# Gating and scattering chunks 18 and 19 inside the retention of a fused retention and mixture-of-experts kernel

## The chip, the cores and the metric

The kernel runs on one core of a Trainium2 chip. The metric is the device time of one execution in microseconds, the median of several runs; lower is better.

## The reference

The program is two layers in a row. A retention layer keeps, for each of 4 batches and 8 heads, a decaying 64 x 64 state over 768 steps; its output, 3072 tokens of 512 features, goes into a mixture of 8 experts in which each token takes the one expert with the largest gate logit.

```python
for t in range(S):                       # B, H, S, D = 4, 8, 768, 64
    state = gamma * state + einsum('bhd,bhe->bhde', k[:, :, t], v[:, :, t])
    y[:, :, t] = scale * einsum('bhd,bhde->bhe', q[:, :, t], state)
x = y.transpose(0, 2, 1, 3).reshape(B * S, H * D)        # 3072 x 512
...
expert_idx = argmax(x @ w_gate, axis=1)                  # 8 experts
for e in range(E):
    xe = x[expert_idx == e]
    out[mask] = gate_w[mask, None] * (maximum(xe @ w1[e], 0) @ w2[e])
```

## The kernel before

The 3072 tokens are 24 chunks of 128 tokens. A loop over n = 0 to 11 takes two chunks, a = 2n and b = 2n + 1, at a time: TensorE (PE) multiplies scores, updates the state and forms the output, VectorE (DVE) masks the scores (`Sb`) and evicts the output (`evict`, tile `xT`), ScalarE (ACT) copies the state (`ub`) and the turned rows (`rows`, tile `xrow`), GpSimd (POOL) scales the values of a later chunk (`scale`, tile `vs`, line 258). Iteration n also makes the gate logits of the two chunks before (`logits`, `finish_logits`).

Chunks are gated in groups, `GROUPS`, each as (first chunk, number). `gating` returns the steps of one group: `choose` finds the best expert on DVE, `soft` and `weights` the gate weight, `rank` counts on PE with small matmuls how many earlier tokens chose the same expert, `slots` turns that into the row of the token in the sorted buffer (`KEY`), `label` writes weight and token number into `xrow` on ACT, `advance` adds the group to the counts that later ranks need. When `KEY` and the label are there, `send_rows` scatters a chunk, one indirect transfer issued by POOL (line 840), into `x_sorted` in DRAM, where each expert's tokens lie together. `BEHIND`, `AMID` and `AFTER` say in which iteration finished chunks are scattered; `send_behind` first copies one column of a tile on POOL (`gated`, line 354), so that POOL goes on only once that tile is written. Between two scatters stands either a `scale` or a `pause`, an idle POOL operation on 256 numbers (line 200). `FULL = 18`: after chunk 17 the expert with the most tokens is known to have enough of them. Its first 256 tokens (`EARLY`) are then fetched (`fetch_early`, tile `xg0`), turned and cut into a high and a low part (`xh0`, `xl0`; the first half of the low part on POOL, line 869). In the code a write to `x_sorted` that stands behind a read of it waits for that read, except where `disjoint` or `declare_no_dep` says otherwise; the scatters are declared free of each other, and of the fetch of the early rows they are not.

The expert weights come as 1 MB pieces (`fetch`, line 136, tile `raw`, two buffers) issued by SyncE (SP) and are split into a high and a low part (`split`, ACT for the high, POOL or DVE for the low part, lines 144 and 145). `SPLITS` places pieces of the first expert's weights in iterations 6, 7, 9, 10 and 11; in 10 and 11 the low parts are POOL's.

After the loop come 32 pieces of the early expert's two products (`early_pieces`, lines 895 and 918; `fill(n)` issues the next n). In their order, with h for a hidden block and r for a result block: h0 h0, then h h r r for each of blocks 1 to 7, then r7 r7. Among them stand, in program order, the rest of the gating, the scatters of the last chunks, the fetch of the late rows (`first["late"]`, the early expert's rows behind the first 256, tile `xg1`), `expert_at[1]`, the first weights `fetch(1, 0)` and the rows of the next expert (tile `buf`). SP then issues `fetch(1, 1)`, waits for POOL's split of `(1, 0)`, issues `fetch(1, 2)`, writes five pads (line 796), loads six registers (line 750) and issues `fetch(1, 3)`. `prep_slices` turns and cuts the late rows on DVE and ACT. Behind that, `moe_main` multiplies the late block (lines 1061 to 1078) and then expert after expert (lines 1164 and 1196). Each engine takes its instructions in the order in which the program issues them.

Of the kernel before, what the change touches and what calls it, by code (L numbers as in the profile page):

```python
# [10 lines left out]
F32 = mybir.dt.float32  # L11
# [8 lines left out]
E, DM, F = 8, 512, 1024  # L20
N = B * S
P = 128
# [21 lines left out]
MAXB = CMAX32 // 32  # L44
WARM = 8
FILL = (1, 3, 4)
GROUPS = ((0, 6), (6, 6), (12, 4), (16, 2), (18, 4), (22, 2))
FULL = 18
BEHIND = {3: (0, 1), 4: (2, 3), 5: (4, 5), 6: (6, 7), 7: (10, 11), 8: (12, 13)}
AMID = {7: (8, 9)}  # L50
AFTER = {8: (14, 15)}
PAUSE = 256
# [54 lines left out]
def retention_moe(ctx, tc, front, qkv, w1, w2, first_rows, second_rows, out):  # L107
# [39 lines left out]
    def region(which):  # L147
        if isinstance(which, int):
            return x_sorted[which]
        return x_sorted[bass.ds(which, 1)].rearrange("o n m -> (o n) m")  # L150
# [47 lines left out]
    def pause():  # L198

        nc.gpsimd.tensor_tensor(out=idle[0:1], in0=cs[0:1, 0:PAUSE], in1=cs[0:1, 0:PAUSE], op=ALU.mult)  # L200
# [19 lines left out]
    with ExitStack() as actx:  # L220
# [6 lines left out]
        ps_1 = apool("ps_1", 1, space=PS)  # L227
# [39 lines left out]
        def bank(i, name, shape=(P, NP, C)):  # L267
            return ps_s.tile(list(shape), F32, name=name, tag=f"s{i}")
# [88 lines left out]
        def send_apart(chunks, between=pause):  # L357
            for i, g in enumerate(chunks):
                if i:
                    between()  # L360
                send_rows(g)

        def send_rows(g):
            b, c = divmod(g, CPB)
            sent = scatter_rows(tc, x_rows, KEY[:, g, 0:1], xrows[b][:, c].rearrange("t q m -> t (q m)"), "sorted")
            if g < GROUPS[0][1]:
                disjoint(tc, sent, "front")
# [18 lines left out]
        def finish_logits(t):  # L386
            i = [n for n, (a, w) in enumerate(GROUPS) if a <= 2 * t < a + w][0]
            a, w = GROUPS[i]
            both = ps_1.tile([P, 2, TW], F32, name="lp", tag="misc")
# [14 lines left out]
        def gating(i):  # L404
            a, w = GROUPS[i]
            total = a + w in (GROUPS[0][1], FULL, NCH)
            last = a + w == NCH
# [4 lines left out]
            NB = w + total  # L412
            v = {}
# [22 lines left out]
                nc.scalar.activation(out=ex[:, :, 0:E], in_=v["sh"], func=AF.Exp)  # L436

            def rank():
                pf = v["pf"] = bank(2, "pf", (P, NB, E)) if i < 3 else ps_1.tile([P, NB, E], F32, name="pf", tag="U" if i == 4 else "misc")
                nc.tensor.matmul(out=pf[:, 0:w, :], lhsT=us, rhs=Eb, start=True, stop=False, skip_group_check=True)  # L440
                for part in [run] + tots:
                    nc.tensor.matmul(out=pf, lhsT=ones, rhs=part.unsqueeze(1).broadcast_to([P, NB, E]),
                                     start=False, stop=False, skip_group_check=True)
                for n in range(NB - 1):
                    nc.tensor.matmul(out=pf[:, n + 1:, :], lhsT=ones,
                                     rhs=Eb[:, n:n + 1, :].broadcast_to([P, NB - 1 - n, E]),
                                     start=False, stop=(n == NB - 2), skip_group_check=True)
# [54 lines left out]
        def fill_rows():  # L502


            assert GROUPS[0][1] * C // E <= 32 * NJ0 - P
            sent = nc.sync.dma_start(out=region(expert_at[0])[32 * NJ0 - P:32 * NJ0], in_=cs[:, 0:ROW])
# [39 lines left out]
        def fill(n):  # L546
            for _ in range(n):
                fn, a = early.pop(0)
                fn(*a)
# [53 lines left out]
        stages = {}  # L603

        for n in range(last + 1):
            a, b = 2 * n, 2 * n + 1
            s = gating(chosen[n]) if n in chosen else None
# [38 lines left out]
            if n == soon:  # L646
                for name in ("slots", "weights", "label", "counts"):
                    s[name]()
                nc.vector.tensor_copy(out=filled, in_=full)
                nc.vector.tensor_scalar(out=s0, in0=full, scalar1=base, scalar2=float(EARLY), op0=ALU.subtract,  # L650
                                        op1=ALU.min)
                nc.vector.tensor_tensor(out=start, in0=s0, in1=base, op=ALU.add)
                send_apart(range(FULL - 2, FULL))
                fill_late()
                fetch_early()
            elif s and n < last:
                s["rank"]()
                s["slots"]()
# [10 lines left out]
            if n == soon - 1:  # L669
                scale(b + 2)  # L670
                scale(a + 4)
            if n in BEHIND:
                send_behind(xTs[n][:, 0, C:C + 1], BEHIND[n], pause if n == soon - 1 else lambda: scale(b + 2))
            if n == 1:
# [19 lines left out]
            if n < last:  # L694
                if n not in BEHIND:
                    scale(b + 2)
# [10 lines left out]
                    load(i)  # L707
        mark_early()

        s = stages[4]  # L710
        fill(FILL[0])
        rows(2 * last, "U", ps_1)
        logits(last)
# [3 lines left out]
        s["rank"]()  # L717
        for name in ("slots", "weights", "advance", "label"):
            s[name]()
        send_apart(range(18, 22))  # L720
        finish_logits(last)
        final = gating(5)
        final["choose"]()
        fill(FILL[2])
        final["soft"]()
# [58 lines left out]
        nc.vector.tensor_scalar(out=mask7, in0=empty, scalar1=float(BIG), scalar2=k_("quad"),  # L784
                                op0=ALU.mult, op1=ALU.add)
        token_mask(0, late, P)
        fill(4)
        prep_slices(nc, nc.vector, xhl1[:, 0], xhl1[:, 1], xt1, xg1, 0, P)
        token_index(0)
        fill(4)  # L790
        for i in range(2):
            split(1, 0, i, nc.gpsimd)
        fetch(1, 2)
# [551 lines left out]
```

## Time and profile before

| | |
|---|---|
| median of 3 runs | 391.99 us (391.64 to 392.82) |
| profiled execution | 394.47 us |
| its span, first to last instruction | 392.7 us |
| mean granted TensorE clock | 0.985 |
| busy: PE, DVE, ACT, POOL | 377.2, 246.3, 140.6, 260.7 us |
| PE busy share of the span | 96% |

Times of instructions are microseconds from the start of the span, so a time in a row is a place in the span. Busy times of different engines lie beside each other and don't add up. The profiled execution is 1.8 us longer than its span; what lies around the span isn't seen in the trace.

### The profile page before, as it was taken

Reading aid. Unit: us, or ns where it says so; the run is one execution under the profiler, and the core shown is the slowest. Engines: PE = TensorE matmul, PEld = TensorE weight load, DVE = VectorE, ACT = ScalarE, POOL = GpSimd, SP = SyncE. Lnnn points to the kernel's source line nnn. Section 1 sums busy time; section 2 is a strip of 40 time slices with the busy share of each in tenths; the row PEclk is TensorE's granted clock in tenths of the full one; section 3 lists DMA queues with packets and bytes.
Section 4 is the critical chain, followed back from the end, with each engine's and each line's share of the span. In section 5 each row is a group of like instructions: output and inputs, shape, how many; then the busy total and the mean of one; then the engine's idle time right before and its main releaser. Section 6 shows DMA issues by size and latency. Waiting matters only on the chain.

```text
span 392.7 us, 8671 instructions
## 1 busy us (share of the span) xinstructions
PE 377.2 (96%) x3272; PEld 352.7 (90%) x3272; DVE 246.3 (63%) x483; ACT 140.6 (36%) x248; POOL 260.7 (66%) x281
## 2 busy tenths in 40 slices
PE   8999999999998998999999999999999999999991
PEld 5887888778997797899999999999999999999881
DVE  3467667765785496675875578386757649667110
ACT  2222334335331463433442353155235325424100
POOL 3752669898480749500699499849929974995874
PEclk9999999999998999899999999999999999999997
DMA  7999999965038979656572764665556455610102
GB/s 300 418 417 415 411 408 420 411 264 165 30 136 207 259 243 272 189 212 131 196 240 65 181 240 140 137 209 167 166 149 223 164 134 201 222 56 17 43 27 76
DMA packets 42030, 82.05 MB, mean 209 GB/s; under 512 B 4267, under 2 KB 17583, under 8 KB 39536
## 3 DMA queue, kind: packets, MB, share of 16 engines
q1 hardware_dynamic: 36656, 67.67, 52.9%
q0 software_dynamic: 5312, 13.49, 9.6%
q8 instruction: 47, 0.77, 0.8%
q14 instruction: 15, 0.12, 0.1%
HBM read 65.80 MB, written 15.82 MB: 208 GB/s over the span
## 4 chain that ended last, share of the span: by engine, by line
PE 69%; DMA 10%; POOL 8%; DVE 6%; issue 3%; SPq 1%; ACT 1%; POOLq 0%; DVEq 0%
PE py L1196 24%; PE ph L1164 23%; PE sp L276 5%; PE Y L326 5%; DMA out<-Z,sidx 4%; POOL out L840 4%; PE tr L346 3%; PE U L291 3%; PE Y L313 3%; DMA buf<-x_sorted 3%; POOL idle L200 2%; DVE wlo L145 2%; PE L L380 2%; DMA raw<-w 2%; DMA head<-first_rows 1%
## 5 line engine op out<-in xcount | busy, mean ns | idle before, releaser
L840 POOL DMA_INDIRECT out<-Z,sidx x88 | 100.6, 1143 | 74.1 <-DVE Z L1043 59.4
L145 DVE TENSOR_TENSOR wlo<-raw,whi 128x1024 fp32r<-128x1024 f32 (+1 forms) x61 | 72.1, 1191 | 14.4 <-ACT whi L144 14.0
L200 POOL TENSOR_TENSOR idle<-cs 1x256 bf16<-1x256 f32 x103 | 75.2, 730 | 2.9
L144 ACT CAST whi<-raw 128x1024 fp32r<-128x1024 f32 (+1 forms) x72 | 67.1, 950 | 11.0 <-DMA raw<-w 11.0
L1196 PE MATMUL py<-hh,whi 128*128 128x392 f32 (+4 forms) x192 | 66.2, 345 | 0.0
L1196 PE MATMUL py<-hh,wlo 128*128 128x392 f32 (+4 forms) x192 | 66.1, 344 | 0.0
L1196 PE MATMUL py<-hl,whi 128*128 128x392 f32 (+4 forms) x192 | 66.0, 344 | 0.0
L1171 ACT ACTIVATE hh<-ph 128x452 fp32r<-128x452 f32 (+6 forms) x56 | 28.3, 507 | 79.2 <-PE ph L1164 78.5
L1164 PE MATMUL ph<-xh,whi 128*128 128x392 f32 (+5 forms) x224 | 49.0, 341 | 2.4 <-DVE hl L1172 2.4
L1172 DVE SCALAR_TENSOR_TENSOR hl<-ph,hh 128x452 fp32r<-128x452 f32 (+6 forms) x56 | 31.9, 572 | 29.6 <-ACT hh L1171 27.9
L1164 PE MATMUL ph<-xl,whi 128*128 128x392 f32 (+5 forms) x224 | 49.6, 343 | 0.0
L1164 PE MATMUL ph<-xh,wlo 128*128 128x392 f32 (+5 forms) x224 | 49.5, 343 | 0.0
L1164 PEld LDWEIGHTS ph<-xh,whi 128*128 128x128 f32 x224 | 40.0, 188 | 3.4 <-DVE hl L1172 3.1
L1164 PEld LDWEIGHTS ph<-xl,whi 128*128 128x128 f32 x224 | 40.8, 190 | 0.2
L1164 PEld LDWEIGHTS ph<-xh,wlo 128*128 128x128 f32 x224 | 40.6, 189 | 0.2
L1196 PEld LDWEIGHTS py<-hh,whi 128*128 128x128 f32 x192 | 36.2, 189 | 0.6 <-DVE Z L1038 0.4
L1196 PEld LDWEIGHTS py<-hl,whi 128*128 128x128 f32 x192 | 36.2, 189 | 0.2
L1196 PEld LDWEIGHTS py<-hh,wlo 128*128 128x128 f32 x192 | 36.2, 189 | 0.2
L279 DVE TENSOR_TENSOR Sb<-sp,cs 128x512 f32<-128x512 f32 x48 | 30.0, 681 | 6.5 <-PE sp L276 6.5
L862 ACT CAST xh<-buf 128x512 fp32r<-128x512 f32 (+7 forms) x26 | 14.4, 556 | 53.9 <-DVE buf L855 53.9
L840 POOL DMA_INDIRECT x_sorted<-xrow,KEY x24 | 25.0, 1041 | 11.3 <-DVE mx L421 5.4
L869 DVE TENSOR_TENSOR xl<-buf,xh 128x512 fp32r<-128x512 f32 (+7 forms) x26 | 17.1, 661 | 13.7 <-ACT xh L862 12.2
(197 smaller groups left out, 557.9 us busy)
## 6 DMA issues: line engine op xcount, KB each, us to landing
raw<-w SPq DMA_DIRECT2D x32, 1024.0 KB
qkv_w<-qkv SPq DMA_DIRECT2D x12, 1024.0 KB, 17.3
qkv_t<-qkv SPq DMA_DIRECT2D x7, 1024.0 KB
qkv_t<-front SPq DMA_DIRECT2D x7, 512.0 KB, 6.3
buf<-x_sorted SPq DMA_DIRECT2D x12, 211.2 KB, 3.8
x_sorted<-cs SPq DMA_DIRECT2D x7, 260.0 KB, 6.5
buf<-x_sorted SPq DMA_DIRECT2D x8, 195.0 KB, 3.6
out<-Z,sidx POOLq DMA_INDIRECT x88
```

The source lines that it names most:

```text
L144: nc.scalar.copy(out=hi[:, h], in_=raw[:, h])
L145: engine.tensor_tensor(out=lo[:, h], in0=raw[:, h], in1=hi[:, h].bitcast(F32), op=ALU.subtract)
L200: nc.gpsimd.tensor_tensor(out=idle[0:1], in0=cs[0:1, 0:PAUSE], in1=cs[0:1, 0:PAUSE], op=ALU.mult)
L276: nc.tensor.matmul(out=sps[r][:, p, :], lhsT=kt[half[r], p, :], rhs=q[half[r], p, :], start=True, stop=True)
L279: nc.vector.tensor_tensor(out=Sb[:, r], in0=sps[r], in1=causal.unsqueeze(1).broadcast_to([P, NP, C]), op=ALU.mult)
L326: nc.tensor.matmul(out=at(Y, g, half[o], r, m), lhsT=vp[:, p, half[r]], rhs=Sb[:, r, p, :], start=(g == 0 and m == 0), stop=True, skip_gro ...
L840: sc = tc.nc.gpsimd.indirect_dma_start(out=dst, out_offset=bass.IndirectOffsetOnAxis(ap=index, axis=0), in_=rows, in_offset=None, bounds_c ...
L869: engine.tensor_tensor(out=xl[:, :, sl], in0=xt[:, :, t0:t0 + w], in1=xh[:, :, sl].bitcast(F32), op=ALU.subtract)
L1164: nc.tensor.matmul(out=ph[:, :w], lhsT=wparts[e, f // 4][a][:, kd, fo:fo + P], rhs=x[:, kd, :w], start=(n == 0), stop=(n == 3 * KD - 1))
L1171: nc.scalar.activation(out=hh[:, :cap], in_=ph[:, :cap], func=AF.Relu)
L1172: nc.vector.scalar_tensor_tensor(out=hl[:, :cap], in0=ph[:, :cap], scalar=0.0, in1=hh[:, :cap].bitcast(F32), op0=ALU.max, op1=ALU.subtract)
L1196: nc.tensor.matmul(out=py[:, :c], lhsT=a[:, f % 4, k * P:(k + 1) * P], rhs=x[:, :c], **se)
```

## The change

Three edits. Group (18, 4) becomes (18, 2) and (20, 2). The first of these is gated in iteration 10, and chunks 18 and 19 are scattered there, behind the eviction of that iteration, with `scale(23)` between them; it was gated in iteration 11 and scattered after the loop. Behind the loop only 20 and 21, and then 22 and 23, are left; since there is one group more, the last one's stage is number 6, and the banks of `rank` are named by the first chunk instead of the number. Before chunk 16 is scattered, a pause is issued. And the preparation of the late rows (`prep_slices`, `token_index`) stands four `fill` pieces earlier: ahead of r4 r4 h6 h6 instead of behind them.

```diff
-GROUPS = ((0, 6), (6, 6), (12, 4), (16, 2), (18, 4), (22, 2))
+GROUPS = ((0, 6), (6, 6), (12, 4), (16, 2), (18, 2), (20, 2), (22, 2))
 FULL = 18
-BEHIND = {3: (0, 1), 4: (2, 3), 5: (4, 5), 6: (6, 7), 7: (10, 11), 8: (12, 13)}
+BEHIND = {3: (0, 1), 4: (2, 3), 5: (4, 5), 6: (6, 7), 7: (10, 11), 8: (12, 13), 10: (18, 19)}
...
-                pf = v["pf"] = bank(2, "pf", (P, NB, E)) if i < 3 else ps_1.tile([P, NB, E], F32, name="pf", tag="U" if i == 4 else "misc")
+                pf = v["pf"] = bank(2, "pf", (P, NB, E)) if a < FULL - 2 or a == FULL else ps_1.tile([P, NB, E], F32, name="pf", tag="U" if a == FULL + 2 else "misc")
...
                 nc.vector.tensor_tensor(out=start, in0=s0, in1=base, op=ALU.add)
+                pause()
                 send_apart(range(FULL - 2, FULL))
                 fill_late()
                 fetch_early()
...
-        s = stages[4]
+        s = stages[5]
...
-        send_apart(range(18, 22))
+        send_apart(range(20, 22))
         finish_logits(last)
-        final = gating(5)
+        final = gating(6)
...
         token_mask(0, late, P)
-        fill(4)
         prep_slices(nc, nc.vector, xhl1[:, 0], xhl1[:, 1], xt1, xg1, 0, P)
         token_index(0)
-        fill(4)
+        fill(8)
```

## Rows read from the trace of the kernel before

**Rows 1.** Who waited for whom, PE alone: us in total, times, longest.

```profile
PE ph L1164 <- DVE hl L1172: 2.4, 2, 1.9
PE acc L918 <- ACT hh L903: 1.4, 1, 1.4
...
PE acc L918 <- DVE hl L904: 0.5, 1, 0.5
```

**Rows 2.** Busy time by stretch: PE, PEld, DVE, ACT, POOL, granted clock, DMA share, GB/s.

```profile
124.80:128.20 3.40, 3.40 (x13) 2.92 (x12) 1.46 (x5) 1.38 (x2) 0.24 (x1) 0.50 1.19 228
...
158.90:162.30 3.40, 3.40 (x12) 3.21 (x11) 0.08 (x1) 0.53 (x2) 3.04 (x4) 0.50 0.96 325
162.30:340.00 177.70, 177.68 (x981) 176.61 (x980) 122.52 (x177) 73.40 (x105) 116.02 (x122) 1.00 0.58 171
```

**Rows 3.** Timeline of POOL, 104 to 116: start, duration, instruction, idle before and releaser.

```profile
104.66 1.01 POOL L840 DMA_INDIRECT x_sorted<-xrow,KEY  x1 [5.39 <-DVE mx L421]
...
106.46 1.01 POOL L840 DMA_INDIRECT x_sorted<-xrow,KEY  x1 [0.16 <-issue]
...
111.92 1.27 POOL L840 DMA_INDIRECT x_sorted<-xrow,KEY  x1 [0.16 <-issue]
...
114.48 1.01 POOL L840 DMA_INDIRECT x_sorted<-xrow,KEY  x1 [0.16 <-issue]
```

**Rows 4.** Timeline of SP's queue, 117 to 145.

```profile
117.38 1.91 SPq L154 DMA_DIRECT2D xg<-x_sorted  x4
...
132.72 0.39 SPq L136 DMA_DIRECT2D raw<-w  x1
...
134.06 6.39 SPq L796 DMA_DIRECT2D x_sorted<-cs  x5
144.42 0.40 SPq L136 DMA_DIRECT2D raw<-w  x1
```

**Rows 5.** Timeline of DVE, 118 to 122.

```profile
118.74 0.15 DVE L212 TENSOR_SCALAR mask<-m 128x1 int32<-128x1 f32 x1
...
121.33 0.71 DVE L855 STREAM_TRANSPOSE xt<-xg 128x512 f32<-128x512 f32 x1 [2.11 <-DMA xg<-x_sorted]
```

**Rows 6.** Timeline of PE, 100 to 124.

```profile
100.46 0.63 PE L895 MATMUL ph<-xl,whi 128*128 128x256 f32 x4
...
120.12 0.28 PE L918 MATMUL acc<-hh,whi 128*128 128x256 f32 x1
...
123.08 0.39 PE L918 MATMUL acc<-hh,whi 128*128 128x256 f32 x1 [1.39 <-ACT hh L903]
```

**Rows 7.** Timeline of DVE, 111 to 113.

```profile
111.54 1.38 DVE L145 TENSOR_TENSOR wlo<-raw,whi 128x512 fp32r<-128x512 f32 x2
```

**Rows 8.** Timeline of DVE, iterations 8, 10 and 11.

```profile
74.01 1.28 DVE L335 TENSOR_TENSOR xT<-Y,buf 128x512 f32<-128x512 f32 x2
...
90.60 1.29 DVE L335 TENSOR_TENSOR xT<-Y,buf 128x512 f32<-128x512 f32 x2 [2.22 <-PE Y L326]
...
98.93 0.88 DVE L869 TENSOR_TENSOR xl<-xt,xh 128x512 fp32r<-128x512 f32 x1
```

**Rows 9.** Timeline of POOL, iterations 8, 10 and 11.

```profile
76.24 1.02 POOL L840 DMA_INDIRECT x_sorted<-xrow,KEY  x1 [0.68 <-ACT ub L294]
...
90.36 1.04 POOL L258 TENSOR_TENSOR vs<-qkv_t,cs 128x512 f32<-128x512 f32 x1
92.01 3.77 POOL L145 TENSOR_TENSOR wlo<-raw,whi 128x512 fp32r<-128x512 f32 x3 [0.62 <-ACT whi L144]
95.96 1.28 POOL L869 TENSOR_TENSOR xl<-xt,xh 128x512 fp32r<-128x512 f32 x1 [0.18 <-ACT xh L862]
```

**Rows 10.** Timeline of DVE, 133 to 143.

```profile
133.44 1.30 DVE L855 STREAM_TRANSPOSE buf<-buf 128x512 f32<-128x512 f32 x2 [0.34 <-DMA buf<-x_sorted]
...
139.85 2.36 DVE L145 TENSOR_TENSOR wlo<-raw,whi 128x1024 fp32r<-128x1024 f32 x2 [0.34 <-ACT whi L144]
```

**Rows 11.** Transfers, 92.8 to 97.0: packets, MB, mean rate, packets by size.

```profile
DMA packets 517, 1.04 MB, mean 248 GB/s; under 512 B 16, under 2 KB 16, under 8 KB 516
```

## The prediction, made before the changed kernel was run

> **What bounds the kernel now.** I read the waits of PE first. PE has work nearly all the time; between the end of the retention and the third expert it stands still in only two places: 1.4 and 0.5 us for the hidden rows of the early expert, and 2.4 us, 1.9 of it in one piece, in the second expert [rows 1]. Next the busy time by stretch: shortly behind each of these two gaps lies a stretch of 3.4 us at a granted clock of 0.50, the lower of the two levels [rows 2]. At full clock half of that time would do, so each costs about 1.7 us. From 162.3 to 340 PE is busy 177.68 of 177.70 us [rows 2]: whatever is won before 162 stays won, and little more can be won there. At stake are 1.9 + 1.7 + 2.4 + 1.7 = 7.7 us.
>
> Then the timelines of POOL and SP, which show what both gaps wait for. POOL scatters six chunks in a row, the first at 104.66 and the last at 114.48 [rows 3]. SP reads the late rows at 117.38, 2.9 us behind the start of the last scatter [rows 4]. DVE, done with its masks at 118.89, stands idle 2.11 us until these rows are there at 121.33 [rows 5]; the hidden rows of block 7 stand behind them on ACT, and PE waits for them until 123.08 [rows 6]. The second gap hangs on the same chain: SP goes on from the late rows to the weights of the next expert, issues their third piece at 132.72, then pads and registers without a rest, and the fourth piece at 144.42 [rows 4]. That is the piece for which the second expert's splits on DVE wait, with the hidden rows `hl` behind them. So the place of the last scatter sets both gaps.
>
> **The change, part by part.** *Two scatters fewer in the tail.* With a pause between, a scatter starts 1.80 us after the one before (104.66 to 106.46 [rows 3]). The last is now the fourth instead of the sixth and starts 3 x 1.80 = 5.4 us behind the first instead of 9.8. Of these 4.4 us, 3.6 are two scatters and two pauses, and 0.8 the slow step from 111.92 to 114.48 (2.56 us instead of 1.80). That step ran beside two low-part splits on DVE, from 111.54 on [rows 7]; chunks 22 and 23 will now be through POOL before those splits begin, so I count the 0.8.
>
> *What is put into iteration 10.* On DVE the choice for two chunks, six operations of some 0.15 us (as the mask at 118.74 [rows 5]), lies in the 2.22 us of idle time ahead of the eviction at 90.60 [rows 8] and costs nothing; without that cover it would be about 1 us. Rank and slots come between the output and the eviction. Their few products and two small DVE operations put the eviction off by 0.65 us, an estimate, so it ends at 90.60 + 0.65 + 1.29 = 92.5. In iteration 8, which has the same order, the scatter came 0.95 us behind the end of the eviction (74.01 + 1.28 to 76.24 [rows 8, 9]), with label and state copy between. That puts scatter 18 at 93.5. It must also wait for the fetch of the early rows, which reads the same buffer. That such a wait is real is seen at the pads: SP issues them at 134.06, just behind the rows of the next expert, which were there by 133.44 [rows 4, 10]. Of the 517 packets from 92.8 to 97.0 only 16 are under 2 KB [rows 11], the rest are weights; so the early rows had landed by 92.8. The new pause ahead of chunk 16 delays their fetch by up to 0.8 (1.80 less 1.01), to 93.6. I take 93.6 for scatter 18. Otherwise the pause costs nothing: DVE turns the early rows only after the masks of iteration 10's scores.
>
> *What is queued behind it on POOL.* Scatter 18 (1.0), the scale of 23 (1.04), scatter 19 (1.0) and issue gaps end at about 96.8. Behind them stand three splits, 3.77 us, and POOL's part of the early rows, 1.28 [rows 9]: done at 101.9 instead of 97.24. PE wants that part at 100.46 [rows 6], or at 100.7 with the products of the rank. It stands still there for about 1.2 us, and all behind it, the rank of 20 and 21 included, is 1.5 us later than before. The splits themselves are wanted only by the hidden blocks from 4 on and are hidden. Bounds: with the scatter at 92.5 the delay is 0.4 us; with both scatters as slow as 1.27 [rows 3] and the eviction and label 0.5 later, 2.5.
>
> One row speaks for a dearer price: the step from 111.92 to 114.48, 0.8 us slow beside the splits on DVE [rows 3, 7]. The Trainium skill (SBUF — State Buffer, section SBUF: two separate sides) has a rule for this: DVE and POOL share a pair of ports, and whichever starts first holds it for its whole instruction, while the other is blocked. By that rule DVE's own part of the early rows, 0.88 us at 98.93 [rows 8], which now falls among POOL's splits, would put POOL off by up to 0.9, and the sum below would be 2.0 instead of 2.9. No row here shows POOL losing time beside that operation, so I stay with 1.5.
>
> *Sum of the scatter chain.* First scatter 1.5 later, last one 4.4 nearer to it: 2.9 us earlier, at 111.6. SP reads the late rows at 114.5, and they are there at 118.4, before DVE is through with its masks. The third and fourth weight pieces could follow 2.9 earlier, at 129.8 and 141.5, since SP has no rest between them.
>
> *Late rows four pieces sooner.* The hidden rows of blocks 6 and 7 now both stand behind the late rows on ACT and DVE. DVE's masks end 1.2 us before PE comes to r6 (118.89 and 120.12 [rows 5, 6]), and both shift alike. From the turning to the release by ACT took 1.75 us (121.33 to 123.08), so r6 waits about 0.5 us, and another 0.5 for its low part, as before [rows 1]: 1.0 instead of 1.9, however early the rows come. Had they not come earlier, the edit would lose: r6 would be released at 123.08, 3.0 us after PE wants it.
>
> PE reaches the late block at + 1.5 (first gap) - 0.9 = + 0.6, or 1.1 us earlier than before if the clock stays up. The rows of the next expert were hardly waited for (0.34 [rows 10]) and come 2.9 earlier. DVE's split of the second piece ended at 142.2 [rows 10]; it moves with PE, to 141.1 or 142.8, and the fourth piece, which needs that buffer, goes at 141.5 or 143.0. Against PE it then comes about 1.8 us sooner than before, and the 2.4 us of the second expert shrink to 0.6 to 1.0.
>
> *Clock.* The two falls of before stand behind gaps of 1.9 us. The gaps forecast are 1.2, 1.0 and up to 1.0; no row tells whether these are enough, so the bounds are none and one fall each. If one stays, the sum is nearly the same wherever it is: in the second expert, the data come 2.9 earlier and the fall is as before, 2.9; at the late rows, the fourth piece goes 1.4 earlier and the second fall is gone, 1.4 + 1.7 = 3.1. I take one, and 2.9.
>
> The rest (one product more in the last rank, choices on two chunks instead of four) is below 0.2 us either way.
>
> Against the profiled execution: 394.47 - 2.9 = 391.6, the span 389.8 and the same 1.8 around it. The median of the runs is 2.5 us below the profiled execution; with the same saving it becomes 391.99 - 2.9 = 389.1 us.
>
> **Rivals.** *Both falls go.* 2.9 + 1.7 = 4.6 us, 387.4. For it: each gap forecast is little more than half of those that had a fall behind them. Against: there are three.
>
> *The gain is held up.* POOL's delay is 2.5, or a fall behind the gap at 100.7 comes on top of another one: the saving is 4.4 - 2.5 = 1.9, or 2.9 - 1.7 = 1.2, or with both nothing. That is 390.1 to 392.0, about 391. For it: DVE ended the second piece's split only 2.2 us before the fourth piece went, so unless PE comes earlier too, the fourth piece can't.
>
> *Slower: POOL is blocked in iteration 10.* Scatter 18 waits for the weight piece behind the early rows, which is through by 97.0 [rows 11], instead of the early rows alone. POOL's part is then ready at 105.3, PE stands still for over 4 us and the clock falls; the delay is 4.9, with 1.4 more for the products of one block at half clock ahead of the rank, and the last scatter comes 4.9 + 1.4 - 4.4 = 1.9 us later: 393.9. It decides from a start of scatter 18 at 96.5 on, where the delay eats the 4.4. Against it: the pads went at 134.06 although the weight piece of 132.72 was still on its way [rows 4].
>
> **How the numbers follow.** Forecast 0.45, both falls gone 0.20, held up 0.25, slower 0.10. The forecast's own range, from delays of 0.4 to 2.5 about the 1.5, is 388.0 to 390.1. Over all cases the range leaves out the slower one and the dear end of the held-up one: 387.0 to 391.4. A measurement of this kernel can't tell 0.3%, 1.2 us, from no change: faster is below 390.8 and slower above 393.2. Faster: 0.45 + 0.20 and 0.06 of the held-up case, 0.71; same: the other 0.19 and 0.02 of the slower one, 0.21; slower 0.08.
>
> **What would show it.** Scatter 18 at about 93.6 and POOL's part of the early rows ending near 102; a PE gap of 1.2 us at 100.7 that waits for it; the tail's scatters from 106.2 to 111.6; the late rows read at 114.5; two PE gaps of 0.5 at r6; the fourth weight piece at 141.5 to 143; at most 1 us of waiting in the second expert, and one stretch at the lower clock. The prediction is wrong if the early rows land after 93.6, if POOL's part is late by more than 2.5 us, or if the fourth piece stays at 144.

## The result and the profile after

The changed kernel is slower: 394.63 us, the median of 4 runs (394.02 to 395.14), against 391.81 us (391.17 to 392.82) for the kernel before, run beside it. The ratio is 1.0078, with an interval from 1.0061 to 1.0094. The prediction of 389.1 us was wrong, and on the wrong side. The profiled execution took 394.56 us, its span 392.8.

The waits of PE in the kernel after: us in total, times, longest. They answer to [rows 1].

```profile
PE ph L895 <- DVE mx L421: 4.0, 1, 4.0
...
PE ph L1164 <- DVE hl L1172: 0.5, 1, 0.5
PE acc L918 <- DVE hl L904: 0.5, 1, 0.5
```

The two waits of before are nearly gone, 1.4 and 2.4 us; a single one of 4.0 has come. The timeline of PE shows its place, and that only one short gap is left at r6 (compare [rows 6]):

```profile
99.94 0.48 PE L895 MATMUL ph<-xh,wlo 128*128 128x256 f32 x2
104.43 0.97 PE L895 MATMUL ph<-xl,whi 128*128 128x256 f32 x4 [4.01 <-DVE mx L421]
...
126.91 0.39 PE L918 MATMUL acc<-hl,whi 128*128 128x256 f32 x1 [0.53 <-DVE hl L904]
```

PE stops in front of the first products that need the low part of the early rows, `xl`. Half of it is computed by POOL, half by DVE. The timeline of POOL after, answering to [rows 3, 9]:

```profile
94.22 1.03 POOL L840 DMA_INDIRECT x_sorted<-xrow,KEY  x1 [2.78 <-ACT whi L144]
...
96.49 1.01 POOL L840 DMA_INDIRECT x_sorted<-xrow,KEY  x1 [0.16 <-issue]
97.53 3.76 POOL L145 TENSOR_TENSOR wlo<-raw,whi 128x512 fp32r<-128x512 f32 x3
101.26 1.25 POOL L869 TENSOR_TENSOR xl<-xt,xh 128x512 fp32r<-128x512 f32 x1
102.48 1.25 POOL L145 TENSOR_TENSOR wlo<-raw,whi 128x512 fp32r<-128x512 f32 x1
110.01 1.00 POOL L840 DMA_INDIRECT x_sorted<-xrow,KEY  x1 [6.28 <-ACT xrow L490]
...
115.43 1.04 POOL L840 DMA_INDIRECT x_sorted<-xrow,KEY  x1 [0.16 <-issue]
```

And that of DVE, answering to [rows 5, 8]:

```profile
97.52 1.29 DVE L335 TENSOR_TENSOR xT<-Y,buf 128x512 f32<-128x512 f32 x2 [2.15 <-PE Y L326]
98.72 5.56 DVE L869 TENSOR_TENSOR xl<-xt,xh 128x512 fp32r<-128x512 f32 x1
104.21 0.16 DVE L421 TENSOR_REDUCE mx<-lp 128x2 f32<-128x16 f32 x1
...
123.92 0.15 DVE L212 TENSOR_SCALAR mask<-m 128x1 int32<-128x1 f32 x1
124.13 0.71 DVE L855 STREAM_TRANSPOSE xt<-xg 128x512 f32<-128x512 f32 x1
```

The second line is the one that matters. The same instruction took 0.88 us before [rows 8]; now it takes 5.56. It starts at 98.72, in the middle of five POOL instructions that follow each other without a rest from 97.53 to 103.73, and it ends at 104.28, 0.55 us behind the last of them. PE goes on at 104.43. The releaser in PE's row is the next DVE instruction, `mx` at 104.21; what PE waited for is the one ahead of it. POOL's own half was ready at 102.51, 1.9 us sooner, so it did not set the gap. It would by itself have made one of 2.1 us, from 100.42 to 102.51; the rest is DVE's half.

The trace of before had a small case of the same kind, though none of the rows above shows it. This split of POOL ran when DVE's half came at 98.93:

```profile
97.98 1.28 POOL L145 TENSOR_TENSOR wlo<-raw,whi 128x512 fp32r<-128x512 f32 x1 [0.74 <-ACT whi L144]
```

It ended at 99.26 and DVE's half at 99.81, the same 0.55 us later. With POOL at rest DVE's half takes 0.68 us (part_gate below), so its 0.88 of before held a wait for POOL already.

What follows from it: the logits and ranks of chunks 20 to 23 stand behind this gap on PE and DVE, so the first scatter of the tail goes at 110.01 instead of 104.66, and the last at 115.43 instead of 114.48. SP's queue moves with it (compare [rows 4]):

```profile
118.35 1.92 SPq L154 DMA_DIRECT2D xg<-x_sorted  x4
...
134.69 6.36 SPq L796 DMA_DIRECT2D x_sorted<-cs  x5
144.99 0.41 SPq L136 DMA_DIRECT2D raw<-w  x1
```

The stretches, answering to [rows 2]; the columns are as there:

```profile
104.60:108.10 3.50, 3.50 (x25) 3.41 (x25) 1.52 (x9) 0.59 (x3) 0.00 (x0) 0.51 0.00 0
124.80:128.20 3.40, 2.81 (x22) 2.40 (x21) 1.62 (x6) 2.06 (x4) 0.00 (x0) 1.00 1.14 287
158.90:162.30 3.40, 3.40 (x20) 3.34 (x19) 1.21 (x3) 1.25 (x2) 3.05 (x4) 1.00 0.95 304
```

The two stretches at the lower level of the clock are gone; one new one stands behind the gap of 4.0. By the profiled executions alone the change would seem neutral, 394.47 against 394.56 us. But the one of before was not a typical one. A second profiled execution of before (the first experiment) took 391.69 us; it had the same gaps and no fall of the clock ahead of 384. Its rows from PE's timeline and from the busy time by stretch (columns of the latter as in [rows 2]):

```profile
121.48 0.38 PE L918 MATMUL acc<-hh,whi 128*128 128x256 f32 x1 [1.36 <-ACT hh L903]
122.51 0.39 PE L918 MATMUL acc<-hl,whi 128*128 128x256 f32 x1 [0.54 <-DVE hl L904]
```

```profile
120.00:124.00 4.00, 2.11 (x15) 1.78 (x14) 2.50 (x7) 0.90 (x2) 0.00 (x0) 1.00 0.90 296
154.00:159.30 5.30, 3.46 (x18) 3.40 (x19) 3.14 (x5) 1.41 (x3) 4.76 (x6) 1.00 1.01 328
```

That this execution is the typical one is seen in the clock too: it has a mean granted clock of 0.993 and the 13 runs of before beside it 0.987 to 0.996, the first profiled one 0.985.

So the comparison with a typical execution of before is, for the gaps named here: + 4.0 for the new gap, + 1.7 for the fall behind it (half of some 3.4 us), - 1.4 at r6 and - 1.8 in the second expert, + 2.5 in all. The executions differ by 2.9 us (391.69 and 394.56). This is no full account of the difference: before_again came to the first products of `xl` at 98.86, 1.56 us ahead of the changed kernel, and other places go the other way.

### The profile page after: what moved, and what is told of

Read it like the earlier page. It is cut to its first block, busy times and chain, and to the rows that moved or that the text cites. A ratio compares the mean times of both kernels' runs of the same rounds, so it can differ in the third digit from the quotient of the medians.

```text
span 392.8 us, 8698 instructions
## 1 busy us (share of the span) xinstructions
PE 375.6 (96%) x3279; PEld 351.7 (90%) x3279; DVE 253.1 (64%) x493; ACT 141.5 (36%) x251; POOL 260.1 (66%) x281
## 4 chain that ended last, share of the span: by engine, by line
PE 46%; DMA 6%; DVE 6%; POOL 6%; issue 3%; ACT 1%; POOLq 0%; DVEq 0%
PE ph L1164 22%; PE py L1196 21%; DMA out<-Z,sidx 4%; POOL out L840 4%; DVE wlo L145 3%; DMA raw<-w 3%; POOL idle L200 2%; PE ph L1061 1%; DVE buf L855 1%; PE acc L918 1%; ACT whi L144 1%; DVE xl L869 1%; PE py L1078 0%; ACT xh L862 0%; DVE Z L1038 0%
## 5 line engine op out<-in xcount | busy, mean ns | idle before, releaser
L840 POOL DMA_INDIRECT out<-Z,sidx x88 | 102.4, 1163 | 74.1 <-DVE Z L1043 59.5
L145 DVE TENSOR_TENSOR wlo<-raw,whi 128x1024 fp32r<-128x1024 f32 (+1 forms) x61 | 73.3, 1210 | 11.3 <-ACT whi L144 10.8
L200 POOL TENSOR_TENSOR idle<-cs 1x256 bf16<-1x256 f32 x102 | 73.7, 722 | 2.9
L1164 PE MATMUL ph<-xl,whi 128*128 128x392 f32 (+5 forms) x224 | 48.8, 340 | 0.0
```

Of the source, the lines that this page charges most:

```text
L145: engine.tensor_tensor(out=lo[:, h], in0=raw[:, h], in1=hi[:, h].bitcast(F32), op=ALU.subtract)
L840: sc = tc.nc.gpsimd.indirect_dma_start(out=dst, out_offset=bass.IndirectOffsetOnAxis(ap=index, axis=0), in_=rows, in_offset=None, bounds_c ...
L1164: nc.tensor.matmul(out=ph[:, :w], lhsT=wparts[e, f // 4][a][:, kd, fo:fo + P], rhs=x[:, kd, :w], start=(n == 0), stop=(n == 3 * KD - 1))
```

## The experiments

There were 18 runs, in five groups; three of them repeat a kernel. Each was compared with runs of the kernel before on its own chip, whose medians were 391.73, 392.81, 393.37 and 393.02 us for the timed groups. Where the edit is "to after", it is made in the changed kernel.

**What held DVE's half.** Four runs. The first is the kernel before, unchanged, for the typical clock.

> The kernel before, unchanged, profiled once more, since its first profiled execution (394.5 us) lay 2.6 us above its median. If that execution was untypical, this one shows about 392 us, a span near 390.2, and one of the two stretches at the lower clock gone, with smaller gaps in the second expert. If the two gaps and two falls belong to the kernel, both are here again and only the time around them differs.

Measured: 391.69 us, described above.

`behind_low`, to after: the two scatters stand behind POOL's half and behind the last split.

```diff
-BEHIND = {3: (0, 1), 4: (2, 3), 5: (4, 5), 6: (6, 7), 7: (10, 11), 8: (12, 13), 10: (18, 19)}
+BEHIND = {3: (0, 1), 4: (2, 3), 5: (4, 5), 6: (6, 7), 7: (10, 11), 8: (12, 13)}
...
             for i in SPLITS.get(n, ()) if n > 7 else ():
                 split(0, *i, nc.gpsimd, 1)
+            if n == last:
+                send_apart((18, 19))
```

> The changed kernel with scatters 18 and 19 moved behind POOL's part of the early rows and its last split in iteration 11. Theory (DVE's part of the early rows was held by POOL's run of operations, and that delay ate the shorter tail): DVE's part is back at 0.9 us instead of 5.56, no PE gap of 4 us at 100.4, first tail scatter at about 105, last at about 110.5, time 388 to 389.5. Rival (the last scatter's place isn't what sets the time): the last scatter comes 4 us earlier and the time stays at 391 or above.

Measured: 387.97 us, ratio 0.9917 (0.9894 to 0.9940). POOL's timeline in this kernel:

```profile
92.74 3.77 POOL L145 TENSOR_TENSOR wlo<-raw,whi 128x512 fp32r<-128x512 f32 x3 [1.39 <-ACT whi L144]
96.45 1.30 POOL L871 TENSOR_TENSOR xl<-xt,xh 128x512 fp32r<-128x512 f32 x1
97.69 1.29 POOL L145 TENSOR_TENSOR wlo<-raw,whi 128x512 fp32r<-128x512 f32 x1
99.13 1.28 POOL L842 DMA_INDIRECT x_sorted<-xrow,KEY  x1
...
109.26 1.04 POOL L842 DMA_INDIRECT x_sorted<-xrow,KEY  x1 [0.16 <-issue]
```

All splits but the last are through before DVE's half comes, at 98.26. It waits for that one only: it takes 1.27 us and ends at 99.53, 0.55 us behind the split's end at 98.98, and PE has no gap there. The last scatter goes at 109.26, the late rows are read at 112.18 and the fourth weight piece is issued at 138.51 (before: 114.48, 117.38, 144.42 [rows 3, 4]). It is faster than both kernels, and gains more than the change was forecast to bring.

`part_first`, to after: POOL's half stands ahead of all four splits.

```diff
-_PIECES = {6: 3, 7: 3, 9: 2, 10: 3, 11: 1}
+_PIECES = {6: 3, 7: 3, 9: 2, 11: 4}
```

> The changed kernel with the three splits of iteration 10 moved behind POOL's part of the early rows, so that POOL's part is ready at about 98.8, and the four splits follow without a rest. Theory (DVE's subtraction with two operands in SBUF gets no turn while POOL's operations follow each other): DVE's part still lasts until about 104, the PE gap stays at 3.5 to 4 us, time 394 to 395. Rival (PE waited only for POOL's part being late, DVE's long duration went with it): the gap is gone, DVE's part takes about 0.9, time 390 to 391.

Measured: 394.68 us, ratio 1.0079 (1.0054 to 1.0105). POOL's half now runs at 97.36 and the four splits from 98.61 to 103.54; DVE's half is held as before:

```profile
98.56 5.54 DVE L869 TENSOR_TENSOR xl<-xt,xh 128x512 fp32r<-128x512 f32 x1
```

PE's gap is 3.99 us. With POOL's half done at 98.65 this excludes the theory that PE waits for POOL's half alone.

`dve_early`, to after: DVE's half is issued right behind the high part, ahead of POOL's run.

```diff
                         cut_high(nc, first["x"][0], first["xt"], j, w)
+                    cut_early(1)
...
-                cut_early()
+                cut_early(0)
```

> The changed kernel with DVE's part of the early rows issued right behind the high parts, ahead of POOL's run of splits. Theory: DVE's part takes at most 1.5 us, from about 95.8, and the PE gap shrinks from 4.0 to the 2.1 us for which POOL's own part is late (102.5 against 100.4); time about 2 us below the changed kernel, 392 to 393. Rival (POOL's lateness alone made the gap): the gap stays at 4.

Measured: 392.77 us, ratio 1.0021 (1.0004 to 1.0038). DVE's half is done at 96.83, and PE's gap shrinks to 2.38 us, now for POOL's half. With DVE's half out of the way, a DVE instruction on 128x8 elements took its place:

```profile
95.72 1.11 DVE L870 TENSOR_TENSOR xl<-xt,xh 128x512 fp32r<-128x512 f32 x1 [0.76 <-ACT xh L863]
...
99.69 4.28 DVE L539 TENSOR_TENSOR empty<-cs,s 128x8 f32<-128x8 f32 x1
```

Over its 4.28 us it does 0.16 us of work; it ends with POOL's run. So a small DVE instruction is held like the large one.

**Can the gain be had otherwise, and which edit does what.** Four kernels, and a fifth from a later group. `part_gate`, to part_first: POOL waits for DVE's half ahead of its splits, by a copy of one column.

```diff
+            if n == last:
+                nc.gpsimd.tensor_copy(out=gated, in_=first["x"][1][:, 0, P:P + 1].bitcast(F32))
             for i in SPLITS.get(n, ()) if n > 7 else ():
```

> The order with POOL's part first, and behind it a one-column copy on POOL that reads DVE's part, so that POOL's four splits wait until DVE has had its turn; nothing else changes, scatters 18 and 19 stay where the changed kernel has them. Theory: POOL rests from about 98.65 until DVE's part ends near 99.4, DVE's part takes about 0.9 us instead of 5.5, the PE gap of 4.0 us shrinks below 0.3, first tail scatter near 105.5 and last near 111, time 388 to 389.5, some 6 us under the same kernel without the copy. Rival (what holds DVE is not POOL's run but the transfers of scatters 18 and 19, which are under way at the same time): DVE's part stays above 3 us, time 393 or more.

Measured: 391.10 us, ratio 0.9955 (0.9931 to 0.9979). DVE's half takes 0.68 us, what it takes with POOL at rest. But the small instructions that follow meet the four splits (POOL, 100.21 to 105.19), and the hidden rows stand behind them; a gap of 2.04 us at 103.56 replaces that of 4.0. I had expected none; the mechanism is the same, its next victim I had not seen:

```profile
99.25 0.68 DVE L871 TENSOR_TENSOR xl<-xt,xh 128x512 fp32r<-128x512 f32 x1
...
100.87 0.65 DVE L539 TENSOR_TENSOR empty<-cs,s 128x8 f32<-128x8 f32 x1
101.56 1.22 DVE L540 TENSOR_SCALAR mask<-empty,cs 128x8 int32<-128x8 f32 x1
```

`before_late`, to before: the third edit alone (late rows four products sooner, as in the diff of the change).

> The kernel before with one edit alone: the late rows prepared four pieces sooner. The prediction's step says that with rows that come no earlier, block 6's hidden rows would be held too: the gaps of 1.4 and 0.5 us in front of block 7's products become about 3.0 and 0.5 in front of block 6's, time 1 to 1.6 us longer, about 393. Rival (the pieces' order is free, since all of them wait for the same rows in the end): no change within 0.5 us.

Measured: 392.76 us, ratio 0.9997 (0.9973 to 1.0022). The gap at r6 grows to 2.82 us, and the second expert's waits shrink to 0.59: without earlier scatters the edit shifts the loss from one place to another. The gap was forecast at about 3.0; the 1 to 1.6 us more in time didn't come.

`behind_low_fill`, to behind_low: the third edit undone.

> The version with scatters 18 and 19 behind POOL's part and its last split, with the late rows prepared at their old place. There the rows land about 2 us before DVE's masks end, and the one gap left ahead of the late block is the 0.53 us at r6 that waits for the low part. Theory (with early rows the sooner place only puts block 6's hidden rows behind them): the gap goes, time 0.5 us shorter, about 387.5. Rival: block 7's hidden rows then wait instead and nothing changes.

Measured: 387.86 us, ratio 0.9883 (0.9850 to 0.9915), not to be told from behind_low. So the third edit is worth nothing that these runs can measure, either way. The second edit was taken out of behind_low in a later group (`behind_low_nopause`).

> The version with scatters 18 and 19 behind POOL's part, without the pause ahead of chunk 16. Theory: the pause moves the early rows by 0.6 us at most, which DVE doesn't wait for; no difference, 387.9 within 0.5. Rival: what the pause delays on POOL shows, 0.6 us shorter.

Measured: 388.85 us, ratio 0.9882 (0.9861 to 0.9903); the intervals overlap, so the pause makes no difference that can be told.

`before_pauses`, to before: six pauses on POOL behind the split of iteration 11, to see whether any POOL work there holds DVE's half.

```diff
                 split(0, *i, nc.gpsimd, 1)
+            if n == last:
+                for _ in range(6):
+                    pause()
```

> The kernel before with six pauses (one partition, 256 numbers each, two operands in SBUF) added on POOL behind its split of iteration 11, where POOL was idle; no scatter is moved. Theory, if any operation of two operands counts: DVE's part at about 98 to 99 lasts until the pauses are through, 4 to 5 us instead of 0.9, a PE gap of 3 us appears, time 394 to 395. Rival (it takes full 128-partition operations, or a run of another kind): DVE's part stays at 0.9 to 1.5, time 391.7.

Measured: 392.52 us, ratio 0.9999 (0.9972 to 1.0026). DVE's half takes 0.88 us; here POOL is late: its first pause takes 1.05 us instead of 0.60. The theory that any run of two-input instructions on POOL holds DVE to its end falls.

**What decides who gets the turn.** First, three more splits in the kernel before, behind that of iteration 11: in `resplit` the quarters 0 to 2 of the same piece are computed a second time, in `resplit_same` three times the last quarter.

```diff
+            if n == last:
+                raw, (hi, lo) = raws[0, 1], wparts[0, 1]
+                for i in (0, 1, 2):
+                    nc.gpsimd.tensor_tensor(out=lo[:, i:i + 1], in0=raw[:, i:i + 1], in1=hi[:, i:i + 1].bitcast(F32), op=ALU.subtract)
```

> The kernel before with POOL's low parts of the second weight piece's first three quarters computed once more, behind its split of iteration 11: three full operations follow that split without a rest, no scatter is moved and no result changes. Theory (a run of full operations on POOL holds DVE's part until its end): POOL's run lasts until about 103, DVE's part 4.5 to 5 us instead of 0.9, a PE gap of about 3 us near 100, the first tail scatter about 3 us later, time 393 to 395.5. Rival (the run alone does nothing; the scatters of 18 and 19 and their transfers are needed for it): DVE's part stays at 0.9, time as before.

> The same three operations of POOL, but all on the last quarter, so that each has to wait for the one before it to be through. If what let DVE through beside the pauses was the rest between dependent operations, DVE's part stays at 0.9 to 1.5 us and the time at that of before. If it was their small size, DVE's part is held here too, 4 us or more.

Measured: 394.80 us, ratio 1.0037 (1.0017 to 1.0057), and 394.16 us, ratio 1.0014 (0.9989 to 1.0040). In both DVE's half got its turn at the first boundary, although splits of full size stood behind it. In resplit, POOL:

```profile
97.83 1.28 POOL L145 TENSOR_TENSOR wlo<-raw,whi 128x512 fp32r<-128x512 f32 x1 [0.74 <-ACT whi L144]
99.06 4.21 POOL L704 TENSOR_TENSOR wlo<-raw,whi 128x512 fp32r<-128x512 f32 x3
```

and DVE:

```profile
98.77 0.88 DVE L873 TENSOR_TENSOR xl<-xt,xh 128x512 fp32r<-128x512 f32 x1
...
100.78 1.28 DVE L539 TENSOR_TENSOR empty<-cs,s 128x8 f32<-128x8 f32 x1
```

The three splits take 4.21 us instead of some 3.76: POOL lost 0.45 to DVE's half. The time isn't that of before, though: in resplit the small instructions are held, one POOL instruction each, and PE waits 0.87 us for `hl` behind them. So the number and the kind of the POOL instructions don't decide alone. A difference that can be read from the program, not from the trace: a split that writes a second time into `wlo` has to wait for an earlier POOL instruction; those of the changed kernel write for the first time and wait only for ACT, which is long done.

`part_break`, to part_first: a pause between POOL's half and the splits.

> The order with POOL's part first and one pause between it and the four splits, in the place of the copy that waits for DVE. If a break of one pause is enough for DVE's turn, DVE's part takes 0.7 to 1.5 us and the PE gap of 4 us near 100 is gone, with a smaller one from later DVE operations among the splits; time 390 to 392. If not, DVE's part stays near 5 us and the time at 394 to 395.

Measured: 395.78 us, ratio 1.0046 (1.0019 to 1.0074). DVE's half came during the pause, at 100.03, and was held through all four splits behind it, 5.81 us. A short instruction in between is no help:

```profile
100.03 5.81 DVE L871 TENSOR_TENSOR xl<-xt,xh 128x512 fp32r<-128x512 f32 x1
```

`held_pauses`, to behind_low, and `held_part_first`, which has the order of part_first besides: POOL is held up by a gated copy and seven pauses instead of the scatters, to see whether these matter.

```diff
+            if n == 10:
+                nc.gpsimd.tensor_copy(out=gated, in_=xTs[n][:, 0, C:C + 1])
+                for _ in range(7):
+                    pause()
```

> The version with scatters 18 and 19 behind POOL's part and its last split, but with POOL held in iteration 10 as the changed kernel holds it: a copy that waits for the eviction, and seven pauses in the place of the two scatters. POOL's run of splits and part then lies at about 98 to 104, under DVE's part, with no scatter ahead of it. Theory A (the run alone holds DVE): DVE's part takes 4 us or more and ends 0.55 behind the run. Theory B (it needs scatters just ahead of the run): DVE's part takes 0.9 to 1.9, it ends within the run, and PE waits only for POOL's late part, some 2.5 us. Time near 391 to 393 under both.

> The same, with POOL's part ahead of the four splits. Theory A: DVE's part is held until the fourth split ends, a PE gap of 3 us or more, 391 to 393. Theory B: DVE's part takes 0.9 to 1.9, PE gap below 1 us, 388 to 390.

Measured: 394.96 us, ratio 1.0036 (1.0007 to 1.0066), and 394.76 us, ratio 1.0050 (1.0017 to 1.0082). DVE's half is held 4.31 us in both. In held_pauses, POOL:

```profile
97.47 3.74 POOL L145 TENSOR_TENSOR wlo<-raw,whi 128x512 fp32r<-128x512 f32 x3
101.18 1.26 POOL L875 TENSOR_TENSOR xl<-xt,xh 128x512 fp32r<-128x512 f32 x1
102.41 1.25 POOL L145 TENSOR_TENSOR wlo<-raw,whi 128x512 fp32r<-128x512 f32 x1
```

and DVE:

```profile
99.90 4.31 DVE L875 TENSOR_TENSOR xl<-xt,xh 128x512 fp32r<-128x512 f32 x1
```

No scatter is needed: that POOL's run is late is enough. DVE's half ends at 104.21, again 0.55 us behind the run's end at 103.66. PE's gap is 2.76 us in both, as it comes later itself, held up ahead of this place by the pauses (it waits 1.1 us for `vs`). The times lie above the 391 to 393 forecast.

**The last group tests the wait.** One run each, so that the traces count here and not the times, with the kernel before at 391.30 us on the same chip. `part_chain`, to part_first: each later split of POOL's run also rewrites the last column of its predecessor, so it has to wait for it.

```diff
         nc.scalar.copy(out=hi[:, h], in_=raw[:, h])
+        if engine is nc.gpsimd and n == 1 and i > 0:
+            lo, raw, hi = (t.rearrange("p a f -> p (a f)") for t in (lo, raw, hi))
+            h = slice(512 * i - 1, 512 * i + 512)
```

> The three later splits of the run on GpSimd each also rewrite the last column of the split before, so that each has to wait for the one before it. Theory wait (VectorE gets its turn where the next GpSimd instruction still has to wait for an earlier one of its own): VectorE's part of the early rows, ready at about 98.6, gets through behind the first split or before it, in 0.9 to 1.4 us instead of 5.54, and TensorE's gap near 100 is under 1 us instead of 3.99. Theory run (the number of two-operand instructions in the run alone decides): held until the end of the run, again 5.5 us or a little more, gap about 4.

Measured: 390.78 us. DVE's half came at 99.16, in front of the first split of the run, which waits for nothing; it was held by that one and got its turn behind it. POOL:

```profile
97.96 1.29 POOL L872 TENSOR_TENSOR xl<-xt,xh 128x512 fp32r<-128x512 f32 x1
99.21 5.71 POOL L148 TENSOR_TENSOR wlo<-raw,whi 128x512 fp32r<-128x512 f32 x4
```

and DVE:

```profile
99.16 1.89 DVE L872 TENSOR_TENSOR xl<-xt,xh 128x512 fp32r<-128x512 f32 x1
...
102.25 1.33 DVE L543 TENSOR_SCALAR mask<-empty,cs 128x8 int32<-128x8 f32 x1
```

1.89 us instead of 5.54, from one column more per split. PE's gap is 0.34 us there and 1.30 behind the small instructions. This is what the theory of the wait expected, but for 0.5 us.

`part_copy`, to part_first: the copy of part_gate, but of a column of POOL's own half, so that it waits only for POOL itself.

> As in the run with the gate, but the one-column copy ahead of the splits reads GpSimd's own part, so that it waits for no other engine. Theory wait: the copy waits for GpSimd's part, which leaves VectorE's part a turn only if that is ready by then (it is not, or barely so: 98.56 against 98.6), so it is held by the splits, about 5 us. Theory gate (what counted in the gated run was that VectorE had its turn before the splits): the same, about 5 us. If instead the copy by itself changes how the splits run, VectorE's part ends within 2 us.

Measured: 390.05 us. I had expected DVE's half to come too late for this copy. It came at 98.53, 0.10 us before POOL's half ended, and went through in 0.68 us, while the copy took 0.56 instead of the 0.18 that it takes in part_gate. The forecast missed; what came agrees with the theory of the wait, in that DVE got in at the one place where POOL waits for itself. POOL and DVE:

```profile
98.69 0.56 POOL L701 COPY gated<-xl 128x1 f32<-128x1 f32 x1
```

```profile
98.53 0.68 DVE L871 TENSOR_TENSOR xl<-xt,xh 128x512 fp32r<-128x512 f32 x1
```

PE's gap of 4.0 us is gone; one of 1.79 stands behind the small instructions, as in part_gate.

`after_again` and `part_gate_again` repeat two kernels, to tell whether it is chance.

> The changed kernel unchanged, to see whether the long hold is the same in another execution. Theory fixed (the order of instructions decides): VectorE's part takes 5.5 us again, gap 4.0. Theory chance (each boundary between two GpSimd instructions is a draw): it ends one to four instructions sooner, 0.9 to 4.3 us.

> The gated kernel unchanged. Theory fixed: the four small VectorE instructions again take one GpSimd split each, 0.65 to 1.3 us, and the gap near 103.6 is 2.0. Theory chance: at least one of them is held for two or more splits, 2.4 us or longer, or gets through within 0.3.

Measured: 393.50 us, with DVE's half held 5.53 us and a gap of 3.98; and 389.22 us, with the four small instructions at 0.65, 1.22, 1.20 and 0.16 us and a gap of 0.91. The long hold came twice, with the same length. Of the small ones three were as in the first execution and the fourth slipped through.

## Why the prediction was wrong, point by point

*What failed.* The step "No row here shows POOL losing time beside that operation, so I stay with 1.5". It asked what DVE's half costs POOL, at most 0.9 us. It never asked what POOL's run costs DVE's half. I had moved that instruction in among POOL's splits in my own sum, and still priced it at its 0.88 us of before, in which a wait for POOL was already hidden. It took 4.7 us more, PE's gap was 4.01 instead of 1.2, and the first scatter of the tail moved by 5.35 us (104.66 to 110.01) instead of 1.5. A smaller part of this is a term that was mis-sized: POOL's own half, for which the sum had the 1.2, would have made a gap of 2.1, and in dve_early, where it is all that is left, the gap is 2.38. That POOL's run is the cause is shown from both sides: with the run out of the way the gap is gone (behind_low), and with only the run delayed, without a scatter, the hold is there (held_pauses). With the scatters where the change has them, and POOL only made to wait for DVE's half, the hold is gone (part_gate, 391.10 against 394.68 us in part_first, each with the kernel before at 392.81 and 391.73). That POOL's half is not what holds PE for 4 us is shown by part_first.

The Trainium skill (SBUF — State Buffer, section SBUF: two separate sides) says that DVE, on an instruction with two inputs in SBUF, and POOL contend for a pair of ports that the first one holds for its whole instruction. The traces agree in kind: in before_pauses POOL's first pause is late behind DVE (1.05 us instead of 0.60), in the changed kernel DVE is late behind POOL. They differ in length: by that rule DVE's half would be held to the end of the POOL instruction then running, at most some 1.3 us here; it was held through the four that followed as well.

*The clock.* I counted two falls of before at stake, from the one profiled execution that I had. The other execution of before has gaps of the same size and no fall, so a gap of 1.9 us need not cost a fall. The median of before lies 2.5 us below the profiled execution, and the clocks of the other runs (0.987 to 0.996, against 0.985) speak against two falls in them. Taking the saving of the profiled execution over to the median was the second mistake: my 2.9 left one fall in the changed kernel, and against an execution of before with none the same sum gives 2.9 - 1.7 = 1.2 us. In the changed kernel one fall was forecast and one came, in both of its profiled executions, but behind the gap of 4.0 and not at the late rows or in the second expert; that the number agrees is luck.

*What held.* Scatter 18 was forecast at 93.6 and went at 94.22. The eviction ahead of it ended at 91.19 and not at 92.5, so it was not the eviction that it waited for; in part_first, where it goes at 94.05, the trace names the fetch of the early rows, the bound that the forecast took. POOL's half was to be done at 101.9 and was at 102.51. What the rank and slots of 18 and 19 cost PE can't be told: it came to the gap at 100.42, in before at 100.46, but kernels whose code is the same up to there came to it at 98.86 (before_again) to 100.74 (resplit_same). From the first to the last scatter of the tail it took 5.42 us, forecast 5.4; the place was 115.43 instead of 111.6, which is the delay again. The late rows are not waited for any more: DVE turns them right behind its last mask (124.13), and r6 loses 0.53 us instead of 1.9, better than the 1.0 forecast. The second expert's waits went from 2.4 to 0.54 us, forecast 0.6 to 1.0, though the fourth piece went at 144.99 and not at 141.5 to 143: PE itself was later. What the change was meant to take away, it took away; it paid for it in iteration 11.

*The rivals.* The slower one named the right side and a gap "over 4 us", by another way: it had scatter 18 go at 96.5 or later, behind a weight piece. It went at 94.22, so that mechanism is refuted; that its 393.9 us lies near the 394.63 measured is luck. The other two did not come about. Behind_low shows what the scatter chain is worth without the hold. It takes away the forecast delay of 1.5 as well, so it answers to the 4.4 of the sum and not to the 2.9: it gained 3.8 us by the medians, without a saved fall of the clock, as the typical execution of before has none to save.

*What stays open.* Where a POOL instruction had to wait for an earlier one of POOL, DVE got its turn: part_chain differs from part_first in one column more per later split, which brings the wait with it, and the hold fell from 5.54 to 1.89 us. It is one run, and a split of 513 columns without the wait was not run beside it. But the small instructions in part_gate and part_copy got through between splits that don't wait for each other, one by one, while the one in dve_early did not. What makes these runs differ isn't settled. One reading that fits and was not tested: in part_gate, part_copy and resplit the POOL instruction right ahead of the splits had itself to wait (for DVE, POOL or ACT), in the six kernels with the long hold POOL came to its run from a scatter, a scale or a pause that stood ready.

## What to carry to other kernels

When work moves on one engine, list what the other engines do at that hour, and price the contention in both directions: a DVE instruction with two inputs in SBUF next to a run of POOL instructions can have the whole run as its price (5.56 us here), not one instruction. Work that was put in front of a critical run is better put behind it (behind_low), or, with a smaller gain here, the run is opened by a real dependence (part_gate, part_chain). Before falls of the clock enter a sum, look at whether the median holds them.

## What the runs showed of the hardware that was not expected

- A run of POOL instructions that all stood ready held a DVE instruction with two inputs in SBUF for 4.3 to 5.8 us, until the run was over, in six kernels (after, part_first, part_break, held_pauses, held_part_first, dve_early); in the last of them it was an instruction on 128x8 elements that takes 0.16 us elsewhere (4.28 us in dve_early).
- A dependence of one column between the POOL instructions cut this from 5.54 to 1.89 us (part_chain); a pause in the run did not (5.81, part_break).
- Small DVE instructions other than tensor_tensor were held too, for one POOL instruction each: the tensor_scalar `mask` 1.22 and the copy `gw` 1.30 us in part_gate, against 0.23 and 0.16 in the changed kernel.
- The two profiled executions of before had gaps of the same size, 1.4 and 1.9 us; one had a fall of the clock behind each of them, the other none.
